# A gated FFN on attention outputs rewritten as a quadratic form in pairs of inducing weights

## The chip, the cores and the metric

The kernel runs on one core of one Trainium2 chip. The metric is the device time of one execution in microseconds (us). In the profile PE is TensorE, PEld its weight loads, DVE is VectorE, ACT is ScalarE, POOL is GpSimd, and SP is SyncE, whose queue issues nearly all DMAs here. L442 is line 442 of the kernel that is profiled.

## The reference

Four batches of 12,416 tokens of 128 features attend to 32 inducing points and back; a gated FFN with 1536 hidden units follows.

```python
h = mab(I, x)                 # 32 x 128 per batch: softmax(I x^T / sqrt(C)) x
x = mab(x, h)                 # per token: a mean of the 32 rows of h with softmax weights
gate = np.maximum(x @ w_gate, 0.0)
val = x @ w_val
return gate * val @ w_out
```

With unnormalized softmax weights p_m and Z = sum of p_m, a token's gate is (sum of p_m G_m)/Z, where G = h w_gate has 32 rows, and its value is (sum of p_m V_m)/Z. All p_m are positive. If the 32 numbers G_m of a unit have one sign, relu is the identity or zero for every token of the batch.

## The kernel before

For each pair of 512-token blocks it makes p by an exponential, then for each of 12 groups of 128 hidden units it forms gate and value by matmuls on p, takes relu on ScalarE, multiplies on VectorE and multiplies by the output weights on TensorE. Scaling by 1/Z^2 goes through a DMA transpose and GpSimd.

```python
        if unit:
            gate = gate_banks(unit)
            for m in unit["mm"][0]:
                gate(*m)                                   # g_ps, PE L910
# ... cut ...
        if unit:
            g16 = unit["g16"] = st([P, 2 * BLK], FP16, "g16", 4)
            w = unit["dst"].shape[-1] // 2
            for k, ps in enumerate(unit["g"]):
                nc.scalar.activation(                      # ACT L1007
                    out=g16[:, k * w : (k + 1) * w], in_=ps[:, 0:w], func=AF.Relu
                )
        if ready:
# ... cut ...
                nc.vector.tensor_tensor(                   # DVE L1019
                    out=dst[:, ks, :], in0=g16[:, ks, :], in1=v[:, ks, 0:w], op=ALU.mult
                )
# ... and in chain(), with the hidden layer as moving operand:
            nc.tensor.matmul(                              # PE L699
                c["ps"][:, 0:w], wo[:, i, :], gv(i), start=(i == 0), stop=(i == NFF - 1)
            )
```

The softmax here doesn't subtract the row's maximum and nothing guards it: scores larger than these inputs give would overflow.

## Time and profile before

| | before |
|---|---|
| time, median of 3 | 698.73 us (698.52 to 698.9) |
| span of the profiled execution | 696.6 us |
| busy PE / DVE / ACT / POOL | 91 / 97 / 97 / 54% |
| granted TensorE clock | 0.9 or more in every slice |

### The profile page before, as it was taken

To read this page: it belongs to the slowest core of one execution; us is meant where nothing else is said; L and a number is where in the kernel's file an instruction comes from. 1 tells how busy PE (TensorE), PEld (TensorE's weight loads), DVE (VectorE), ACT (ScalarE), POOL (GpSimd) and SP (SyncE) were. 2 spreads that over 40 slices of the span, in tenths; PEclk is the share of its full clock that TensorE was granted. 3 is DMA by queue.
4 is the path that set the end of the run, shared out by engine and by line. 5 is a ranking of instruction groups with operands and counts; after the bars stand their busy time and mean duration, and the time that the engine had idled before them with its cause. 6 is when DMAs were issued, how large, how long until landed. Compare 5 with 4: busy or idle time off the path is not lost.

```text
span 696.6 us, 14008 instructions
## 1 busy us (share of the span) xinstructions
PE 633.8 (91%) x4581; PEld 180.6 (26%) x4581; DVE 676.7 (97%) x617; ACT 672.4 (97%) x1381; POOL 372.7 (54%) x681
## 2 busy tenths in 40 slices
PE   7999998999999999989999999998999888888997
PEld 5422222222222222222222222222222222222224
DVE  4799999999999999999999999999999999999997
ACT  5799999999999999999999999999999999999996
POOL 4729746654277554756257473873434543534443
PEclk9999999999999999999999999999999999999999
DMA  9667778531666857513186785632223132232222
GB/s 349 220 133 188 165 170 168 106 99 47 149 163 172 203 139 158 144 50 89 54 204 165 204 175 151 129 93 70 69 76 85 52 92 58 79 90 49 77 56 92
DMA packets 142634, 87.58 MB, mean 126 GB/s; under 512 B 117184, under 2 KB 125664, under 8 KB 140256
## 3 DMA queue, kind: packets, MB, share of 16 engines
q1 hardware_dynamic: 142368, 86.60, 49.1%
q8 instruction: 36, 0.59, 0.3%
q14 instruction: 38, 0.31, 0.2%
q10 hardware_dynamic: 192, 0.08, 0.0%
HBM read 27.80 MB, written 25.43 MB: 76 GB/s over the span
## 4 chain that ended last, share of the span: by engine, by line
ACT 40%; PE 25%; issue 19%; DVE 13%; DMA 1%; SPq 1%; ACTq 0%; POOL 0%; DVEq 0%
ACT g L1007 30%; DVE gv L1019 13%; PE o_ps L699 11%; PE v_ps L910 8%; ACT oT L705 6%; PE g_ps L910 3%; ACT p2q L201 2%; ACT p1T L558 2%; DMA gv<-in_x_dram 1%; PE o_ps L766 1%; ACT hgv L176 1%; SPq L87 1%; PE h_ps L624 0%; PE xT_ps L275 0%; PE idle_ps L269 0%
## 5 line engine op out<-in xcount | busy, mean ns | idle before, releaser
L1019 DVE TENSOR_TENSOR gv<-g,v_ps 128x1024 f16<-128x1024 f16 (+1 forms) x578 | 657.2, 1209 | 3.4 <-ACT g L1007 1.0
L1007 ACT ACTIVATE g<-g_ps 128x512 f16<-128x512 f32 (+1 forms) x1168 | 603.2, 618 | 6.5 <-PE g_ps L910 2.3
L699 PE MATMUL o_ps<-gv,wo 128*128 128x512 f16 x1128 | 352.4, 384 | 46.0 <-ACT oT L705 45.8
L716 POOL TENSOR_SCALAR osb<-o,z2i 128x128 f32<-128x128 f16 x380 | 165.2, 452 | 223.1 <-DMA o<-oT 212.6
L910 PE MATMUL g_ps<-p,hgv 32*128 32x512 f16 x1152 | 282.4, 379 | 0.8 <-ACT g L1007 0.5
L910 PE MATMUL v_ps<-p,hgv 32*128 32x512 f16 x1152 | 223.6, 384 | 5.5 <-DVE gv L1019 4.3
L910 PEld LDWEIGHTS <-hgv 32*128 32x128 f16 x2400 | 66.7, 91 | 267.3 <-issue 263.0
L699 PEld LDWEIGHTS <-wo 128*128 128x128 f16 x1176 | 80.8, 97 | 212.4 <-issue 198.6
L455 POOL TENSOR_TENSOR z2i<-zt,minus 128x16 f32<-128x16 f32 (+3 forms) x31 | 73.4, 2369 | 0.5
L705 ACT CAST oT<-o_ps 128x512 f16<-128x512 f32 (+1 forms) x98 | 59.1, 603 | 0.1
L526 POOL CAST x<-x 128x2048 f16<-128x2048 f32 x18 | 34.1, 1894 | 13.9 <-DMA x<-in_x_dram 13.9
L448 POOL TENSOR_TENSOR zt<-zt 128x32 f32<-128x32 f32 (+5 forms) x124 | 35.0, 282 | 9.7
L448 POOL TENSOR_TENSOR zt<-p2T 128x256 f32<-128x256 f16 (+3 forms) x31 | 17.5, 563 | 33.5 <-DMA p2T<-p2q 20.9
L602 POOL TENSOR_TENSOR zq<-p1g 128x256 f32<-128x256 f16 x18 | 12.1, 672 | 6.5 <-DMA p1g<-p1T 6.5
L276 DVE COPY xT<-xT_ps 128x1024 f16<-128x1024 f16 (+1 forms) x15 | 8.6, 583 | 6.8 <-PE xT_ps L275 6.7
L285 POOL CAST x<-gv 128x512 f16<-128x512 f32 (+2 forms) x15 | 8.5, 564 | 10.3 <-DMA gv<-in_x_dram 10.3
L201 ACT ACTIVATE p2q<-s_ps 128x512 f16<-128x512 f32 x22 | 13.4, 610 | 0.0
L604 POOL TENSOR_TENSOR zq<-zq 128x256 f32<-128x256 f32 x15 | 10.9, 726 | 1.2
L558 ACT ACTIVATE p1T<-s1T_ps 128x512 f16<-128x512 f32 x18 | 11.0, 611 | 0.0
L185 PE MATMUL s_ps<-xT,hT 128*32 128x512 f16 x108 | 10.8, 389 | 0.1
L287 ACT CAST x<-gv 128x512 f16<-128x512 f32 (+2 forms) x15 | 7.1, 495 | 3.9 <-DMA gv<-in_x_dram 3.9
L275 PE MATMUL xT_ps<-eye,x 128*128 128x128 f16 x97 | 8.2, 219 | 2.1 <-DVE x L282 0.7
(97 smaller groups left out, 163.8 us busy)
## 6 DMA issues: line engine op xcount, KB each, us to landing
out_dram<-osb SPq DMA_DIRECT2D x95, 256.0 KB, 2.2
x<-in_x_dram SPq DMA_DIRECT2D x18, 1024.0 KB, 5.9
p<-p2q SPq DMA_DIRECT2D x88, 64.0 KB, 2.0
gv<-in_x_dram SPq DMA_DIRECT2D x9, 512.0 KB, 6.7
o<-oT SPq DMA_TRANSPOSE x98, 2.4
gv<-in_x_dram SPq DMA_DIRECT2D x6, 256.0 KB, 9.1
x<-in_moe_w_out_dram SPq DMA_DIRECT2D x1, 768.0 KB, 8.8
x<-in_moe_w_gate_dram SPq DMA_DIRECT2D x1, 512.0 KB, 6.0
```

Source lines behind the costliest of these rows:

```text
L201: nc.scalar.activation(out=p2q, in_=ps, func=AF.Exp, scale=sm_scale)
L448: nc.gpsimd.tensor_tensor(out=dst, in0=v[:, :, :, 0:m], in1=v[:, :, :, m : 2 * m], op=ALU.add)
L455: nc.gpsimd.tensor_tensor(out=z2i, in0=v[:, :, :, 0], in1=minus1[:, 0 : n * g].rearrange("p (n g) -> p n g", n=n), op=ALU.pow,)
L526: nc.gpsimd.tensor_copy(out=s["x16"][:, t0:t1, :], in_=s["x32", q])
L558: nc.scalar.activation(out=p1T, in_=ps, func=AF.Exp, scale=sm_scale)
L602: add(out=z, in0=s["p1g"][q][:, 0:half, :], in1=s["p1g"][q][:, half:, :], op=ALU.add)
L699: nc.tensor.matmul(c["ps"][:, 0:w], wo[:, i, :], gv(i), start=(i == 0), stop=(i == NFF - 1))
L705: nc.scalar.copy(out=oT[:, 0:w], in_=c["ps"][:, 0:w])
L716: nc.gpsimd.tensor_scalar(out=osb[:, t, :], in0=o16[:, t, :], scalar1=zz, scalar2=zz, op0=ALU.mult, op1=ALU.mult,)
L910: nc.tensor.matmul(ps[:, cols], hgv[:, s * P : (s + 1) * P], p2, start=True, stop=True)
L1007: nc.scalar.activation(out=g16[:, k * w : (k + 1) * w], in_=ps[:, 0:w], func=AF.Relu)
L1019: nc.vector.tensor_tensor(out=dst[:, ks, :], in0=g16[:, ks, :], in1=v[:, ks, 0:w], op=ALU.mult)
```

## The change

For a unit of one sign, relu(gate) times value is a sum over pairs (m, m') of p_m p_m' G_m V_m' / Z^2. A pair weight is one exponential: p_m p_(m+k) = exp(score_m + score_(m+k)), and the sum of two scores is one score against h_m + h_(m+k). So the kernel makes F, 512 pair weights per token (16 shifts k of 32 inducing points), multiplies it with one table T of 512 rows and 129 columns per batch (the last column gives Z^2), and divides once. T is the sum over the units with positive gate of (G_m V_m' + G_m' V_m) times the output weights: products of 768 elements on VectorE into U[0] and U[1], a "join" U[0] + U[1] on GpSimd, and 12 matmuls for each quarter of T. The 16 pairs of shift 16 and up to 16 unsure units go into a fifth block. If more than 16 units are unsure or the sign bound is too wide, a general path recomputes all in a branch.

One slot is one block of 512 tokens; a batch has 24 and a last tile of 128. Work for the next batch (load, cast, transpose, narrow scores, largest |x| for the bound, h, gates, products, tables) is laid over these slots.

```diff
-            for k, ps in enumerate(unit["g"]):
-                nc.scalar.activation(
-                    out=g16[:, k * w : (k + 1) * w], in_=ps[:, 0:w], func=AF.Relu
-                )
# ... cut: all of the hidden layer, its output chain, the transposed way out ...
+        act.activation(
+            out=F[g][:, 2 * half : 2 * half + 2, :], in_=ps, func=AF.Exp, scale=sm_scale
+        )
# ... cut ...
+        for j in range(4):
+            nc.tensor.matmul(
+                ps, F[g][:, j, tok], T[b % 2][:, j, 0 : P + 1], start=j == 0, stop=False
+            )
# ... cut: the fifth block, then per three tiles one reciprocal and one product, and a store ...
+    def products(i, t0, nt, odd):
+        dve.tensor_tensor(
+            out=U[i][:, t0 : t0 + nt, k0:NS:2, :],
+            in0=a[:, t0 : t0 + nt, 0:M].unsqueeze(2).broadcast_to([P, nt, nk, M]),
+            in1=shifted(w, 0, t0, nt, k0 - odd, 2, nk),
+            op=ALU.mult,
+        )
+    def joined(eng, t0, nt):
+        eng.tensor_tensor(
+            out=U[0][:, t0 : t0 + nt, 1:, :],
+            in0=U[0][:, t0 : t0 + nt, 1:, :],
+            in1=U[1][:, t0 : t0 + nt, 1:, :],
+            op=ALU.add,
+        )
# ... cut: the order of the next batch's loads on SyncE, casts on GpSimd, transposes on SyncE ...
+            at = (first + 2 * q) if b > 1 else min(-1, 2 * q - 13)
+            task(at, load, "S")
+            task(at + 3 if b > 1 else at, cast, "S")
+            task(max(at + 5, base - 2 + q) if b > 1 else at, transp, "S")
# ... cut: the products of the next batch, and after every four of them a join ...
+            ops += [lambda i=i, t0=t0, odd=odd: products(i, t0, 3, odd) for i in (0, 1) for odd in (0, 1)]
+            ops.append(lambda t0=t0: joined(pool, t0, 3))
# ... cut ...
+    left = quadratic_kernel(tc, *args)
+    with tc.If(left > 0):
+        general_kernel(tc, *args)
```

## The prediction

> **What bounds the kernel now.** I read the busy table first, then the costliest groups, then one undisturbed stretch by engine.
>
> ```profile
> PE 633.8 (91%) x4581; PEld 180.6 (26%) x4581; DVE 676.7 (97%) x617; ACT 672.4 (97%) x1381; POOL 372.7 (54%) x681
> ...
> L1019 DVE TENSOR_TENSOR gv<-g,v_ps 128x1024 f16<-128x1024 f16 (+1 forms) x578 | 657.2, 1209 | 3.4 <-ACT g L1007 1.0
> L1007 ACT ACTIVATE g<-g_ps 128x512 f16<-128x512 f32 (+1 forms) x1168 | 603.2, 618 | 6.5 <-PE g_ps L910 2.3
> L699 PE MATMUL o_ps<-gv,wo 128*128 128x512 f16 x1128 | 352.4, 384 | 46.0 <-ACT oT L705 45.8
> ```
>
> DVE and ACT are both at 97% with about 5 us of idle: both are full, and they are full of one thing, the hidden layer. Per pair of 512-token blocks DVE does 12 products of 1024 (657.2/578 = 1.14 us each) and ACT 24 relus of 512 (603.2/1168 = 0.52 us each). PE is not the limit. So time falls only if these elements disappear, and both engines must lose them. The change does that.
>
> ```profile
> 300.00:313.60 13.60, 12.26 (x108) 3.52 (x108) 13.59 (x13) 13.29 (x29) 6.74 (x10) 1.00 0.23 65
> ```
>
> That is a steady stretch (stretch, then busy us and instructions of PE, weight loads, DVE, ACT, GpSimd, then clock, DMA share, GB/s): DVE is busy 13.59 of 13.60 us at clock 1.00. The new work is priced from the order of time near the end (start, length) and from the groups by shape (busy us, mean ns):
>
> ```profile
> 689.45 1.29 PE L766 MATMUL o_ps<-wo,gv 128*128 128x128 f16 x20
> ```
>
> ```profile
> L196 ACT ACTIVATE p<-s_ps 128x512 f16<-128x512 f32 x5 | 3.0, 609 | 1.7 <-PE s_ps L185 1.7
> L296 ACT ACTIVATE p<-s_ps 128x128 f16<-128x128 f32 x6 | 1.6, 276 | 1.6 <-PE s_ps L294 1.6
> L779 DVE TENSOR_TENSOR osb<-o_ps,zz 128x384 f32<-128x384 f32 x1 | 0.6, 557 | 0.5 <-PE o_ps L766 0.5
> L319 DVE TENSOR_REDUCE z1s<-z1a_ps 128x32 f32<-128x256 f32 x1 | 0.4, 414 | 0.0
> ```
>
> Twenty matmuls of 128 columns, each with its weight load, take 1.29 us (0.22 latency, then 56 ns each); an exponential's slope (609-276)/384 = 0.87 ns an element; an output eviction of three tiles 557 ns; a reduction of 256 in 414 ns.
>
> **What the Trainium skill says.** "VectorE: DVE Perf Modes", section on the perf-mode tier table: tensor_tensor runs at two elements a cycle on 16-bit SBUF operands, one with a PSUM operand, and tensor_reduce always at one. The trace agrees for PSUM (1024 in 1.14 us) and one reduction; no fp16 SBUF product is in it. "ScalarE: Activation LUTs", section "What ACT_TABLE_LOAD costs": 186 ns + 0.833 N, back-to-back overlapping by about 93 ns, whatever the function. The trace has 609 ns for 512 and 0.52 us start to start: it agrees, so an exponential of 1024 is an estimated 1.04 us, 0.95 us start to start. "TensorE: Matmul & The Clock Gate", section on 56 ns: N/2.4 + 2.5 ns; 56 ns measured here. "Runtime: NRT & Kernel Launch", section "Instruction fetch mechanics": a taken branch to a far target stalls for a fetch; no line of this trace shows it.
>
> **The change, part by part.** Does the general path run? I worked out the test on the reference's inputs: bound 0.0036 (limit 0.0625), 761 to 775 of 1536 units certainly on, the rest certainly off, none unsure (limit 16). So the branch is not taken; the general path costs only the test.
>
> Removed: all of the hidden layer's L1007, L1019 and L699 work, the transposed output path through DMA and GpSimd (380 scalings, 165 us) and GpSimd's sums of exponentials.
>
> Added, per slot of one 512-token block (24 and a rest tile per batch, 100 slots):
> - ACT: two exponentials of 128x1024, 2 x 0.95 = 1.9 us; a 512 one every fourth slot, 0.13. About 2.0.
> - PE: four score matmuls of 512 at 0.216 and twenty of 129 at 0.056: 0.86 + 1.13 = 2.0; unsure units, still computed in full, an estimated 0.17. About 2.2.
> - DVE: per three tiles a reciprocal (estimated 0.17 and 0.1 of dependence) and the 557 ns eviction, 0.77 start to start, so 1.03 a slot; unsure units, 13 passes of 512 from PSUM at 0.62 per batch, 0.3. About 1.35.
>
> So PE sets a plain slot, 2.2 us: 55 us for a batch with nothing else. Added per next batch, laid over 24 slots:
> - PE: 97 x 3 narrow matmuls at about 28 ns = 8 us; tables 60 x 56 ns = 3.4; gates and small ones 2. Total 2.2 x 24.25 + 13, about 66 us.
> - ACT: six exponentials and eight gate copies, some 8 us: about 58 in all.
> - DVE: the largest |x|, 12 reductions of 1024 at about 1.15 = 14 us; 16 products of 768 at 0.49 (two a cycle) = 8; masked output weights 1.7; sums, signs, masks 7. With 25 for outputs and 8 for unsure units, about 62.
>
> The means nearly balance, but they bunch. In slots 1 to 6 DVE holds 1.03 + 2.3 + 0.2 and often 0.62: about 3.9 us against PE's 3.3. In slot 10 ACT has 1.9 + 2.6 of gate copies; in slots 11 and 12 DVE has about 4.7. PE takes everything in order with two output banks, so it cannot hide a peak. Slot by slot: slot 0 2.2; slots 1 to 6 23.4; 7 to 9 2.8 + 2.2 + 2.7; 10 to 13 4.5 + 4.7 + 4.7 + 3.4; 14 to 17 10 (products beside outputs); 18 to 22 14.3 (2.2 and 0.7 for a table each); 23 and 24 4.2; sum 79. Perfect smoothing would give 66. Two output banks hold 1.5 slots, so I choose a value between, nearer the peaks: 74.
>
> Prologue. hT was ready at 23.66 us. The built order puts nine reductions of 1024 (10 us) among DVE's turn copies; DVE was busy 9.3 us of the first 20, so it becomes full there: I add 3 us. Then six more reductions (4 us), sums of h, 16 products (8), bound, signs, masks (5) in one DVE chain, then table, evictions and the first unsure-unit block (6): first output near 51 us.
>
> Batch 1's arrival. Here I expect the largest loss. In the built order SyncE's queue holds load 0, transpose 0, load 1, transpose 1 and so on, and each transpose waits for GpSimd's cast of that load. GpSimd's first cast stands behind the unsure-unit work, which waits for the signs: near 45 us.
>
> ```profile
> x<-in_x_dram SPq DMA_DIRECT2D x18, 1024.0 KB, 5.9
> ...
> xT<-x SPq DMA_TRANSPOSE x18, 4.4
> ```
>
> (DMA issues: KB each, median us to landing; then min/median/max ns of issuing a transpose, of a cast, and the queue's own waits: us in total, times, longest.)
>
> ```profile
> L532 SPq DMA_TRANSPOSE xT<-x x18: 1622/1927/2347, 36.8 to 444.8; - x18
> ```
>
> ```profile
> L526 POOL CAST x<-x x18: 1891/1894/1897, 31.7 to 440.7; 128x2048 f16<-128x2048 f32 x18
> ```
>
> ```profile
> SPq L709 <- ACT g L1007: 253.8, 94, 6.3
> ```
>
> The last line shows the queue standing on one entry's wait. One round is 5.6 (load) + 1.9 (cast) + 1.9 (issuing the transpose) = about 9.5 us. Transposes 0 to 5 issue at 47, 56.5, 66, 75.5, 85, 94.5 and the rest tile near 99; they land 3 to 4 us later. Slot 1+q has in-order score matmuls on chunk q, so slot 7 begins at about 102, not at 51 + 2.2 + 23.4 = 77: some 25 us of PE standing. Later batches issue transposes one per slot, three slots ahead, and escape.
>
> Sum: 102 + slots 7 to 24 of batch 0, 48 (74 less the 25.6 of slots 0 to 6) + two batches of 74 + a last batch with no successor and no scores in its last five slots, 51 + last store, register loads and branch 6 = about 355; the time reported is 2 above the span (698.7 against 696.6): 356.
>
> **The rivals.**
> 1. The arrival chain is hidden or shorter: the first load has long landed, later loads in quiet queues take under 5 us. Against: the median of 5.9 us in a kernel with less store traffic at that point, and the queue order. If hidden, 356 - 25 = about 331.
> 2. PE is fed perfectly (two output banks and exponentials five slots ahead absorb the peaks): batches at 66 instead of 74, about 332; together with rival 1, 310. For it: the means. Against: one in-order PE stream, and only two banks of each kind.
> 3. DVE takes PE's place entirely: fp16 products at one a cycle (0.87 us), reductions slower beside GpSimd's 18 casts. Batches of 82, the prologue 6 us longer: about 385.
> 4. The branch is taken, or the jump costs tens of us. The inputs speak against; the first would at least double the time.
>
> **Range and chances.** 356 with errors of about 7 in the prologue, 10 in the chain and 6 per batch: 325 to 385. The removed work is over 600 us on each of two engines and the added under 270 on any, so faster is nearly certain; only a taken branch would undo it.
>
> **What would show it.** Right: exponentials of 1024 at about 1.04 us mean, 192 of them; 1552 matmuls on F 56 ns apart; first output near 51 us; PE idle in gaps of 5 to 8 us between 55 and 102, released by a DMA landing in xT; clock below 1 there; slots of about 4 us in which DVE is full at the start of batches 1 and 2; 2.2 us slots with PE full in batch 3. Wrong: PE idle on F or on ACT throughout would mean ACT is the limit; reductions far from 1.15 us or products far from 0.5 us would move each batch; a gap after the last store would be the branch.

## More of the kernel before

The page also cuts the span into 40 equal slices and gives the busy tenths of each, 9 for 90% or more. Here they are for DVE and ACT:

```profile
DVE  4799999999999999999999999999999999999997
ACT  5799999999999999999999999999999999999996
```

After a prologue of two slices both engines are full to the end.

## The result

The changed kernel is correct and takes 408.58 us (median of 4; 407.4 to 409.88), the kernel before 698.62 us (698.38 to 698.9) in the same rounds. The ratio is 0.585 (95% interval 0.583 to 0.586). A ratio is the mean time of one kernel's fast runs over the mean time of the other's fast runs of the same rounds, so it is not quite the ratio of the medians quoted. The direction was right, but 408.6 lies above the predicted range of 325 to 385, and 52.6 us over the predicted 356.

From the page of the kernel after: busy shares, slices, then the costliest groups (busy us, mean ns of one | idle just before, and its releaser).

```profile
PE 331.0 (81%) x4358; PEld 230.9 (57%) x4358; DVE 273.5 (67%) x581; ACT 245.5 (60%) x350; POOL 115.9 (28%) x148
...
PE   5874785455696798999996689999996799999993
...
PEclk9696699666689868999998888999998999999998
...
L642 ACT ACTIVATE F<-e_ps 128x1024 f16<-128x1024 f32 x192 | 194.6, 1032 | 90.6 <-PE e_ps L635 83.7
L656 PE MATMUL o_ps<-T,F 128*128 128x129 f16 x1552 | 144.1, 231 | 15.1 <-DVE osb L675 14.8
...
L675 DVE TENSOR_TENSOR osb<-o_ps,rzo 128x384 f32<-128x384 f32 x132 | 72.5, 549 | 7.8 <-DMA out_dram<-osb 3.2
...
L783 DVE TENSOR_REDUCE xmp<-xT 128x1 f32<-128x1024 f16 x36 | 42.1, 1210 | 22.8 <-DMA xT<-x 22.8
```

Both engines that were full have lost over half of their work (DVE from 676.7 to 273.5 us busy, ACT from 672.4 to 245.5), and the prices of the new pieces came as predicted: 192 exponentials of 1024 at 1.03 us, the eviction at 0.55 us, the reduction at 1.21 us. No engine is full on the average. But the slices of PE swing between 4 and 9, and those of its granted clock with them, down to 6: the kernel has stages with different bounds, and the misses are in them. A table by stretch (PE busy, PEld, DVE, ACT, POOL, each with its instructions; granted clock; DMA share; GB/s) separates these stages:

```profile
60.00:114.00 54.00, 31.94 (x477) 23.45 (x476) 23.33 (x38) 18.52 (x22) 9.76 (x6) 0.73 0.58 154
...
178.70:207.00 28.30, 27.02 (x508) 20.38 (x506) 24.96 (x46) 19.89 (x26) 0.00 (x0) 1.00 0.63 142
207.00:241.00 34.00, 27.13 (x291) 17.39 (x289) 28.60 (x60) 21.05 (x31) 18.11 (x19) 0.85 0.55 192
...
365.00:390.00 25.00, 25.00 (x289) 16.60 (x287) 13.57 (x34) 22.85 (x25) 0.00 (x0) 1.00 0.30 116
```

The last row is the last batch, which has no successor: PE is busy 25.00 of 25.00 us at clock 1.00, so PE sets a plain slot, as predicted. Dated by its first matmul on F, such a slot takes 2.04 us without matmuls for the unsure units and 2.45 us with them (three slots of four), 2.35 us on the mean, where the prediction had 2.2. The second row is the first nine slots of batch 1: PE nearly full again. The first row is slots 0 to 6 of batch 0, with PE busy for 31.94 of 54 us at a granted clock of 0.73. The third row is slots 9 to about 15 of batch 1, where most of the products and joins for batch 2 stand: 34 us, PE's work stretched by a clock of 0.85, and GpSimd at work for 18.11 us. The list of waits names what PE waited for in the bad rows (us in total, times, longest):

```profile
PE s_ps L774 <- DMA xT<-x: 21.9, 5, 5.1
...
PE o_ps L656 <- DVE osb L675: 14.8, 8, 3.0
...
PE pos_ps L507 <- DVE row L505: 10.1, 3, 3.4
...
DVE oh L520 <- POOL pm L518: 9.9, 4, 2.7
```

**The first stage.** The narrow scores wait for turned tokens of batch 1. The chain of waits between 54 and 80 us (start, length, what) shows the loop behind it:

```profile
56.66 1.95 SPq L766
...
58.71 5.75 DMA x<-in_x_dram
...
64.51 1.90 POOL x L762
...
66.43 1.71 SPq L766
...
68.24 5.92 DMA x<-in_x_dram
```

SyncE issues a transpose (L766), only then the next load, then stands until GpSimd has cast it: 5.75 + 1.90 + 1.71 and a few hundredths, 9.5 us a round. This is the arrival chain of the prediction, with its predicted period.

**The third stage.** This is the order of time within slots 10 to 15 of batch 1 (start, length, engine, line, operation; in brackets what ended the idle time before):

```profile
226.72 1.89 POOL L762 CAST x<-x 128x2048 f16<-128x2048 f32 x1
226.85 2.17 DVE L442 TENSOR_TENSOR U<-ga,vb 128x768 f16<-128x768 f16 x1
...
231.95 0.61 PE L656 MATMUL o_ps<-T,F 128*128 128x129 f16 x4 [3.05 <-DVE osb L675]
...
233.00 1.06 PE L635 MATMUL e_ps<-xT,hs 128*128 128x512 f16 x2
...
234.00 3.15 POOL L450 TENSOR_TENSOR U<-U,U 128x1440 f16<-128x1440 f16 x1
...
234.31 3.25 DVE L442 TENSOR_TENSOR U<-va,gb 128x768 f16<-128x768 f16 x1
```

A product takes 0.55 us when it stands alone (ten us earlier in the same batch). Beside the cast it takes 2.17, beside the join 3.25, and both times it ends 0.41 us after GpSimd does: 226.72 + 1.89 = 228.61 against 226.85 + 2.17 = 229.02, and 237.15 against 237.56. It is as if the product only begins when GpSimd ends. The whole trace says the same: each of the 23 products that take over 0.65 us began after a GpSimd instruction had, and ended 0.37 to 0.42 us after that one's end. The eviction behind it comes late, PE stands 3.05 us for the output bank, and its two score matmuls take 1.06 us where they take 0.59 elsewhere. The Trainium skill says just this: "SBUF — State Buffer", section "Who interferes with whom", has GpSimd and VectorE share a pair of ports, a VectorE instruction with two SBUF inputs contend with a GpSimd instruction that reads SBUF, and the second one to issue blocked until the first finishes. Its exceptions agree with the trace too: the evictions, which read PSUM, stay at 0.56 us.

| stage | predicted | measured | difference |
|---|---|---|---|
| start to slot 7 of batch 0 | 102 | 114.5 | +12.5 (9.7 of it before the first eviction, at 60.7 instead of 51) |
| slots 7 to 24 of batch 0 | 48 | 64.2 | +16.2 |
| batch 1 | 74 | 88.5 | +14.5 |
| batch 2 | 74 | 83.4 | +9.4 |
| last batch, and the rest to the reported time | 59 | 59.3 | 0.3 |

Slot 7 is dated by its first narrow score, a batch from first eviction to first eviction (from the reciprocal that opens it). The measured column adds up to the 409.9 us of the profiled run, the predicted one to 357, which the prediction rounded to 356.

### The profile page after: what moved, and what is told of

It is laid out like the page before. It is cut to its first block, busy times and chain, and to the rows that moved or that the text cites.

```text
span 407.7 us, 10298 instructions
## 1 busy us (share of the span) xinstructions
PE 331.0 (81%) x4358; PEld 230.9 (57%) x4358; DVE 273.5 (67%) x581; ACT 245.5 (60%) x350; POOL 115.9 (28%) x148
## 4 chain that ended last, share of the span: by engine, by line
PE 46%; DVE 22%; DMA 9%; POOL 7%; ACT 7%; issue 5%; SPq 3%; DVEq 0%; POOLq 0%; ACTq 0%
PE o_ps L656 16%; PE e_ps L635 12%; DMA x<-in_x_dram 7%; DVE U L442 5%; ACT F L642 4%; PE o_ps L660 3%; DVE osb L675 3%; SPq L766 3%; PE hz_ps L795 3%; POOL x L762 3%; DVE xmp L229 3%; PE gv_ps L714 3%; POOL U L450 2%; PE T_ps L488 2%; ACT p L778 2%
## 5 line engine op out<-in xcount | busy, mean ns | idle before, releaser
L642 ACT ACTIVATE F<-e_ps 128x1024 f16<-128x1024 f32 x192 | 194.6, 1032 | 90.6 <-PE e_ps L635 83.7
L656 PE MATMUL o_ps<-T,F 128*128 128x129 f16 x1552 | 144.1, 231 | 15.1 <-DVE osb L675 14.8
L656 PEld LDWEIGHTS <-F 128*128 128x128 f16 x1552 | 109.6, 102 | 49.4 <-DVE osb L675 18.9
L635 PE MATMUL e_ps<-xT,hs 128*128 128x512 f16 x384 | 122.5, 405 | 4.6 <-DVE hs L375 3.9
L660 PE MATMUL o_ps<-T,gmv 128*128 128x129 f16 x388 | 88.5, 228 | 0.1
L675 DVE TENSOR_TENSOR osb<-o_ps,rzo 128x384 f32<-128x384 f32 x132 | 72.5, 549 | 7.8 <-DMA out_dram<-osb 3.2
L450 POOL TENSOR_TENSOR U<-U,U 128x1440 f16<-128x1440 f16 x12 | 35.9, 2991 | 131.1 <-DVE U L442 72.1
L783 DVE TENSOR_REDUCE xmp<-xT 128x1 f32<-128x1024 f16 x36 | 42.1, 1210 | 22.8 <-DMA xT<-x 22.8
L762 POOL CAST x<-x 128x2048 f16<-128x2048 f32 x18 | 34.5, 1928 | 44.7 <-DMA x<-in_x_dram 44.5
L660 PEld LDWEIGHTS <-gmv 128*128 128x128 f16 x388 | 40.1, 103 | 0.7 <-DVE gmv L730 0.2
L635 PEld LDWEIGHTS <-hs 128*128 128x128 f16 x384 | 31.8, 102 | 8.8 <-DVE hs L375 4.0
L720 DVE TENSOR_SCALAR g<-gv_ps 128x512 f16<-128x512 f32 (+1 forms) x28 | 17.7, 630 | 15.5 <-PE gv_ps L714 15.3
L774 PE MATMUL s_ps<-indT,xT 128*128 128x32 f16 x288 | 10.2, 180 | 21.9 <-DMA xT<-x 21.9
L706 ACT ACTIVATE p<-s_ps 128x512 f16<-128x512 f32 (+1 forms) x28 | 15.6, 558 | 2.6 <-PE s_ps L697 2.6
L442 DVE TENSOR_TENSOR U<-ga,vb 128x768 f16<-128x768 f16 x16 | 16.7, 1043 | 0.0
```

Of the source, the lines that this page charges most:

```text
L442: dve.tensor_tensor(out=U[i][:, t0 : t0 + nt, k0:NS:2, :], in0=a[:, t0 : t0 + nt, 0:M].unsqueeze(2).broadcast_to([P, nt, nk, M]), in1=shif ...
L450: eng.tensor_tensor(out=U[0][:, t0 : t0 + nt, 1:, :], in0=U[0][:, t0 : t0 + nt, 1:, :], in1=U[1][:, t0 : t0 + nt, 1:, :], op=ALU.add,)
L635: nc.tensor.matmul(ps[:, d, :], hs[:, j * P : (j + 1) * P], xTs(s["xT"], n * TPB, TPB), start=True, stop=True,)
L642: act.activation(out=F[g][:, 2 * half : 2 * half + 2, :], in_=ps, func=AF.Exp, scale=sm_scale)
L656: nc.tensor.matmul(ps, F[g][:, j, tok], T[b % 2][:, j, 0 : P + 1], start=j == 0, stop=False)
L660: nc.tensor.matmul(ps, gmv[b, n // 4][rows, tok], T[b % 2][rows, 4 + r, 0 : P + 1], start=False, stop=True,)
```

## The experiments

My theory after the result had four parts, for four places: (1) the arrival chain of batch 1 costs some 25 us; (2) in slots 10 to 18 products of two fp16 SBUF operands stand still while GpSimd works; (3) the position matmul waits behind VectorE work; (4) the prologue is long because of the 15 big reductions for the largest |x|. The rival for 2 is that VectorE is simply full there, or that GpSimd's own queue is too long; for 3, that the wait only moves. Each edit is against the changed kernel.

| run | median us (range) | ratio to before | batches 0, 1, 2 (us) |
|---|---|---|---|
| the changed kernel | 408.58 (407.4–409.88) | 0.585 | 117.9, 88.5, 83.4 |
| e1_loads_ahead | 384.68 (383.25–385.43) | 0.550 | 93.4, 88.5, 83.4 |
| e2_no_join | 397.63 (396.67–398.8) | 0.570 | 111.9, 82.8, 82.7 |
| e3_casts_later | 400.63 (399.94–401.34) | 0.573 | 112.0, 84.7, 85.0 |
| e4_row_first | 409.32 (408.69–409.94) | 0.586 | 117.8, 88.6, 83.6 |
| e5_no_largest | 399.66 (399.17–401.44) | 0.572 | 117.3, 88.5, 83.4 |
| e6_no_join_casts_later | 393.12 (392.46–394.49) | 0.563 | 110.5, 81.6, 80.7 |
| e7_relu_on_act | 404.84 (402.44–407.61) | 0.578 | 117.6, 88.6, 82.2 |
| e8_joins_after | 413.44 (412.73–414.01) | 0.592 | 118.3, 88.9, 87.0 |
| e8b_joins_last | 388.83 (388.64–390.48) | 0.557 | 110.0, 81.2, 79.4 |
| e10_joins_on_dve | 401.16 (399.54–403.01) | 0.574 | 115.3, 86.0, 80.1 |
| e12_no_join_tables_late | 397.8 (395.0–400.65) | 0.571 | 111.7, 83.3, 81.2 |
| e9_all | 369.93 (369.27–373.83) | 0.531 | 86.0, 81.6, 81.9 |
| e11_all_row_first | 365.26 (364.26–366.47) | 0.522 | 85.0, 80.2, 80.2 |
| e13_all_joins_last | 365.41 (365.23–366.47) | 0.524 | 85.5, 80.8, 78.3 |
| e14_all_joins_last_casts_later | 370.91 (370.76–371.71) | 0.531 | 86.5, 84.8, 79.5 |

Each row has four runs over three rounds, all correct, with the kernel before at 698.5 to 698.7 beside them. The batches are those of the profiled run, which can lie up to 3 us from the median (e7: 407.61, e12: 395.0). From its first reciprocal to its last, the last batch took 50.5 us in every one.

### e1_loads_ahead: the arrival chain taken apart

```diff
@@ -753,3 +753,3 @@
         first = base - 14
-        task(first, begin, "S")
+        task(first if b > 1 else -30, begin, "S")
         for q in range(NCH):
@@ -806,6 +806,11 @@
 
-            at = (first + 2 * q) if b > 1 else min(-1, 2 * q - 13)
-            task(at, load, "S")
-            task(at + 3 if b > 1 else at, cast, "S")
-            task(max(at + 5, base - 2 + q) if b > 1 else at, transp, "S")
+            at = first + 2 * q
+            if b > 1:
+                task(at, load, "S")
+                task(at + 3, cast, "S")
+                task(max(at + 5, base - 2 + q), transp, "S")
+            else:
+                task(-29 if q < 3 else 2 * q - 33, load, "S")
+                task(2 * q - 28, cast, "S")
+                task(2 * q - 28, transp, "S")
             task(base + 1 + q, score, "B")
```

> Batch 1's first three loads are issued before the first transpose, so a round of the SyncE queue no longer holds a load's flight. Theory (the arrival chain stalls the PE by 28.8 us: slot 0 to the last score takes 53.8 us in batch 0 against 25.0 in batch 1): rounds shrink from 9.7 to about 4 us, the last chunk's scores come near 90 instead of 114, and the time falls by 20 to 29 us to about 380 to 388. Rival (the chain hides another wait, such as output banks or stores held behind the transposes): less than 10 us.

Measured: 384.68, 24 us less, all in batch 0 (117.9 to 93.4 us). The wait for turned tokens falls from 21.9 to this line in the list of waits:

```profile
PE s_ps L774 <- DMA xT<-x: 4.3, 2, 2.5
```

Part 1 holds. The same loads, casts and transposes run; only their order on SyncE differs. The predicted 25 us was right in kind and size.

### e2_no_join, e3_casts_later, e6_no_join_casts_later: GpSimd's work taken away from the products

e2 leaves the joins out: TensorE sums both halves of U, 24 matmuls a quarter table instead of 12.

```diff
@@ -486,6 +486,11 @@
         ps = bank("m", "T_ps", [P, P])
-        for t in range(NFF):
-            nc.tensor.matmul(
-                ps, u_cols(0, t, j), won[:, t, :], start=t == 0, stop=t == NFF - 1
-            )
+        for i in range(2):
+            for t in range(NFF):
+                nc.tensor.matmul(
+                    ps,
+                    u_cols(i, t, j),
+                    won[:, t, :],
+                    start=(i, t) == (0, 0),
+                    stop=(i, t) == (1, NFF - 1),
+                )
         act.copy(out=T[b % 2][:, j, 0:P], in_=ps)
@@ -841,3 +846,3 @@
             ops += [lambda i=i, t0=t0, odd=odd: products(i, t0, 3, odd) for i in (0, 1) for odd in (0, 1)]
-            ops.append(lambda t0=t0: joined(pool, t0, 3))
+            ops.append(lambda: None)
         for k, f in enumerate(ops):
```

> GpSimd's sum of the two product tables (12 of 3.0 us) is gone; the PE adds both tables in PSUM instead, 48 more matmuls of 56 ns per batch, 2.7 us. Theory (a DVE product with two fp16 operands in SBUF cannot proceed while GpSimd works, so the join stretches the product beside it to 1.7 to 3.3 us and the in-order PE stands behind DVE): products beside no other GpSimd work take 0.55 us, the oh step no longer waits 2.7 us for GpSimd, and each of three batches loses some 4 to 8 us: 385 to 397. Rival (DVE's peak of work alone stalls the PE, and GpSimd only fills time that is there anyway): the time rises by up to 8 us for the added matmuls, or stays.

e3 keeps the joins and starts the loads of batches 2 and 3, and so their casts, some slots later, behind the products.

```diff
@@ -806,3 +806,3 @@
 
-            at = (first + 2 * q) if b > 1 else min(-1, 2 * q - 13)
+            at = (base - 10 + q) if b > 1 else min(-1, 2 * q - 13)
             task(at, load, "S")
```

> Loads and GpSimd casts for batches 2 and 3 move out of the slots in which DVE makes the products; nothing is added or removed. Theory of the shared access: the products that were stretched to 2.2 us by a 1.9 us cast go back to 0.55, some 2 to 5 us in each of batches 0 and 1: 400 to 405. Rival (peak of DVE alone): no change within 2 us.

e6 has both edits.

> No joins and the casts out of the product slots. If both act through the same exclusion the gains of 11 and 8 us add up, 389 to 392, and nearly all products of batches 1 to 3 take 0.55 us; if one of them had only uncovered the other's idle time, it stays at 395 or above.

Measured: 11.0, 8.0 and together 15.5 us less. The groups by shape of e6 show the products back near their price (busy us, mean ns):

```profile
L442 DVE TENSOR_TENSOR U<-va,gb 128x768 f16<-128x768 f16 x16 | 10.1, 629 | 0.0
...
L442 DVE TENSOR_TENSOR U<-ga,vb 128x768 f16<-128x768 f16 x16 | 9.7, 606 | 0.0
```

In the changed kernel these two read 972 and 1043 ns. The batches fall from 88.5 and 83.4 to 81.6 and 80.7 us. This speaks for part 2 but doesn't prove it: the edits also shorten GpSimd's queue, and e2 gives TensorE 144 more matmuls. The two gains add up to 19, of which 15.5 came. The product times themselves nearly add: the four groups by shape sum to 57.8 us in the changed kernel, 44.7 in e2, 51.4 in e3 and 39.0 in e6. Why the time gains less is open.

### e8_joins_after and e8b_joins_last: the same instructions, parted in time

A clean test keeps every instruction and changes only what stands beside what. e8 puts the four joins after the last products in the order of issue.

```diff
@@ -841,2 +841,3 @@
             ops += [lambda i=i, t0=t0, odd=odd: products(i, t0, 3, odd) for i in (0, 1) for odd in (0, 1)]
+        for t0 in range(0, NFF, 3):
             ops.append(lambda t0=t0: joined(pool, t0, 3))
@@ -847,3 +848,3 @@
         for j in range(4):
-            task(c + 10 + j, lambda j=j: table(b, j), "B")
+            task(c + 11 + j, lambda j=j: table(b, j), "B")
         task(c + 9, lambda: table5(b), "B")
```

> The same instructions as the changed kernel, but GpSimd's four joins per batch stand behind all products, in slots that have none (tables one slot later). It separates GpSimd's work from its being at the same time as DVE's products, without the 2.7 us of matmuls that the run without joins adds. Theory (products and GpSimd exclude each other): time falls by 6 to 12 us, to 397 to 403, products beside no join at 0.55 us. Rival (the run without joins gained because work was removed from a chain of GpSimd): less than 3 us of gain or a loss.

Measured: 413.44, 4.9 us more. The expectation fell, and the order of time shows why:

```profile
233.68 9.50 POOL L450 TENSOR_TENSOR U<-U,U 128x1440 f16<-128x1440 f16 x3
...
234.04 3.25 DVE L442 TENSOR_TENSOR U<-ga,vb 128x768 f16<-128x768 f16 x1
...
237.21 3.20 DVE L442 TENSOR_TENSOR U<-va,ga 128x672 f16<-128x672 f16 x1
...
241.15 0.62 PE L656 MATMUL o_ps<-T,F 128*128 128x129 f16 x4 [6.46 <-DVE osb L675]
```

A join waits only for its own products. The first three had all been released, so GpSimd ran them back to back for 9.50 us while VectorE still had its last products: two in a row of over 3 us, and PE standing 6.46 us. The edit had not parted the work, it had packed it. For e8b the order of the joins is reversed: the one that needs the last products stands first in GpSimd's queue and holds the others back.

```diff
@@ -841,2 +841,3 @@
             ops += [lambda i=i, t0=t0, odd=odd: products(i, t0, 3, odd) for i in (0, 1) for odd in (0, 1)]
+        for t0 in range(9, -1, -3):
             ops.append(lambda t0=t0: joined(pool, t0, 3))
@@ -847,3 +848,3 @@
         for j in range(4):
-            task(c + 10 + j, lambda j=j: table(b, j), "B")
+            task(c + 13 + j // 2 + j % 2, lambda j=j: table(b, j), "AB"[(j + 1) % 2])
         task(c + 9, lambda: table5(b), "B")
```

> The second try at parting the joins of the product tables from the products in time, with every instruction kept. All four joins (four additions of 1440 fp16 elements a row on GpSimd, 2.99 us each) now stand after the last products, and the one of the last products stands first, so that none can start before VectorE is done with them; the tables come two or three slots later. By the theory that a VectorE product of two fp16 operands from SBUF cannot go on while GpSimd works on SBUF: no product beside a join is over 0.7 us, TensorE no longer waits 3 to 6 us for a table eviction there, and the time falls from 408.6 to between 396 and 403 (leaving the joins out gave 397.6). By the rival, that leaving the joins out helped because GpSimd had 12 us less to do in a batch (its masks, positions and casts stand behind the joins in its queue): nothing is gained, 406 to 414.

Measured: 388.83, 19.8 us less, more than the theory's range. Here the joins follow the last product:

```profile
228.38 0.55 DVE L442 TENSOR_TENSOR U<-va,gb 128x768 f16<-128x768 f16 x1
...
229.02 11.53 POOL L450 TENSOR_TENSOR U<-U,U 128x1440 f16<-128x1440 f16 x4 [3.21 <-DVE U L442]
```

PE's wait for evictions falls from 14.8 to 5.6 us in the list of waits. All 581 VectorE and 148 GpSimd instructions are still there, and GpSimd is as busy as before (115.6 against 115.9 us); only the overlap with the joins is gone. The casts still stretch one product in batch 0 and two in batch 1, to 1.6 or 2.0 us. The edit also packs the products closer and moves the tables, but e8 has the same packing and was slower, and e12 below gives the tables the same late slots for nothing. From e8 to e8b only the order of the joins turns and the tables move, and the time falls by 24.6 us. The rival of the long GpSimd queue predicted 406 to 414 and falls, and part 2 is shown.

### e10_joins_on_dve and e12_no_join_tables_late: the rivals of 388.8

e10 lets VectorE do the joins.

```diff
@@ -841,3 +841,3 @@
             ops += [lambda i=i, t0=t0, odd=odd: products(i, t0, 3, odd) for i in (0, 1) for odd in (0, 1)]
-            ops.append(lambda t0=t0: joined(pool, t0, 3))
+            ops.append(lambda t0=t0: joined(dve, t0, 3))
         for k, f in enumerate(ops):
```

> The joins of the product tables done by VectorE instead of GpSimd: four additions of 1440 elements a batch for batches 1 to 3. [...]one takes 0.55 us times 1440/768, about 1.0 us, 4 us more of VectorE in a batch, and GpSimd loses 12. By the theory of exclusion the products are back at 0.55 us beside them and TensorE has its 12 matmuls a table instead of 24, so most of the 11 us that leaving out the joins gave should come: 396 to 402. By the rival, that in these slots VectorE is simply full and any work on it counts, the added 12 us of VectorE eat the gain: 406 to 412.

Measured: 401.16, 7.4 us less, inside the theory's range. The added VectorE work (12 joins of 0.95 us) costs less than the blocked products did, but it isn't free: batch 1 takes 86.0 us where e2 has 82.8. Part of what the rival says may thus be true as well. But the products, too, are longer than in e2 (48.7 us in all against 44.7), as casts still meet them, so how full VectorE is in these slots isn't shown.

e12 asks why e8b beat e2. It is e2 with the tables in e8b's late slots (the line of e8b's diff that moves the tables, added to e2).

> No joins, as in the run that gave 397.6, but the tables in the late slots of the run that gave 388.8. If the parting in time made the 388.8 and the late slots of the tables nothing, this stays near 397.6 (395 to 400), and what separates it from 388.8 is the 144 further table matmuls of TensorE, 144 x 56 ns = 8 us. If the late tables made it, this falls to 386 to 391.

Measured: 397.8 (with a wide 395.0 to 400.65), the same as e2's 397.63. The late slots give nothing by themselves. What separates e2 and e12 from e8b is TensorE's 144 further matmuls at 56 ns, an estimated 8 us, against 8.8 us measured.

### e4_row_first: the position matmul

VectorE's row of unsure units was put before the masked output weights (1.75 us), so that TensorE's position matmul, which stands in order ahead of other work, need not wait for both.

```diff
@@ -431,2 +431,5 @@
         )
+
+    def masked_wo(b):
+        on = state[b]["on"]
         dve.tensor_tensor(
@@ -492,3 +495,3 @@
 
-    def positions(b):
+    def rows(b):
         s = state[b]
@@ -503,4 +506,8 @@
         )
-        row = mt([P, 1], FP16, "row", 1)
+        row = s["row"] = mt([P, 1], FP16, "row", 1)
         dve.tensor_copy(out=row, in_=s["cum"][:, NFF - 1 : NFF])
+
+    def positions(b):
+        s = state[b]
+        row = s["row"]
         ps = bank("m", "pos_ps", [P, 2])
@@ -835,3 +842,5 @@
         task(c + 3, lambda: masks(b), "A")
+        task(c + 3, lambda: rows(b), "A")
         task(c + 3, lambda: positions(b), "B")
+        task(c + 3, lambda: masked_wo(b), "B")
         task(c + 4, lambda: chosen(b), "A")
@@ -874,2 +883,4 @@
     masks(0)
+    masked_wo(0)
+    rows(0)
     table_all(0, 0, 3)
```

> The masked output weights (1.75 us on DVE) move behind the row counts that a PE matmul waits for; the same work in all. Theory (the PE, in order, stands 3.4 us at the position matmuls of each batch): that wait falls to about 1 us and each of three batches gains 2 to 3 us: 400 to 404. Rival (DVE is full there, so the wait comes back at the next output eviction): within 2 us of 408.

Measured: 409.32, no gain. The wait for the row fell from 10.1 to 5.5 us, and PE's wait for evictions rose from 14.8 to 19.8 us. Part 3 fell and its rival was right: the wait only moved to the evictions. e11 below fits this: there, with the products no longer blocked, the same edit pays.

### e5_no_largest: the price of the reductions

This is a measurement of cost: the largest |x| is replaced by a constant that covers the data, so the result stays correct, but the kernel would not be safe for other data.

```diff
@@ -227,10 +227,3 @@
         def largest(j):
-            t0, t1 = parts[j]
-            nc.vector.tensor_reduce(
-                out=xmp[:, j : j + 1],
-                in_=xTs(xT, t0, t1 - t0).rearrange("p t c -> p (t c)"),
-                axis=AX.X,
-                op=ALU.max,
-                apply_absolute_value=True,
-            )
+            nc.vector.memset(xmp[:, j : j + 1], 0.6)
 
@@ -782,9 +775,3 @@
                     m = n // 2 if n > 1 else 1
-                    dve.tensor_reduce(
-                        out=s["xmp"][:, 2 * q + h : 2 * q + h + 1],
-                        in_=s["xT"][q][:, h * m : (h + 1) * m, :].rearrange("p t c -> p (t c)"),
-                        axis=AX.X,
-                        op=ALU.max,
-                        apply_absolute_value=True,
-                    )
+                    dve.memset(s["xmp"][:, 2 * q + h : 2 * q + h + 1], 0.6)
 
```

> The largest |x| is not computed but set to a constant of 0.6, a cost measurement only: the general test is lost, the output stays right for these inputs. DVE loses 48 reductions of 1.13 us and 6 of 0.6, 58 us. Theory: in the prologue DVE is full from 9 to 52 us, so the first eviction comes 8 to 12 us earlier (49 to 53 instead of 60.7); in slots 1 to 6 of batches 1 and 2 the PE takes over at 3.3 us a slot from about 3.5, so 1 to 3 us each; in batch 0 nothing more, the arrival chain holds it: 393 to 400. Rival (the prologue's end is set by GpSimd's chain for the fifth table and not by DVE): the first eviction moves by less than 4 us and the time stays above 402.

Measured: 399.66, 8.9 us less. The first eviction comes at 53.1 instead of 60.7 us, and batches 1 and 2 stay as they were (88.5, 83.4). So the reductions cost 7.6 us in the prologue and nothing in slots 1 to 6, where the prediction had made VectorE the limit at 3.9 us a slot: PE is the limit there, as the row 178.70:207.00 above shows. (The page has 45 reductions of 1024 elements, not the 48 expected.)

### e7_relu_on_act: a small shift from VectorE to ScalarE

```diff
@@ -719,10 +719,3 @@
             p2s[b, q, "g"] = mt([P, BLK], FP16, "g16", 2)
-            dve.tensor_scalar(
-                out=p2s[b, q, "g"][0:k, 0:w],
-                in0=ps[0:k, 0:w],
-                scalar1=0.0,
-                scalar2=1.0,
-                op0=ALU.max,
-                op1=ALU.mult,
-            )
+            act.activation(out=p2s[b, q, "g"][0:k, 0:w], in_=ps[0:k, 0:w], func=AF.Relu)
         else:
```

> The maximum with zero of the unsure units goes from DVE (24 of 0.69 us) to ACT. Theory (DVE's sum of work in slots 1 to 6 and 10 to 16 stalls the PE): each batch with a successor gains 1 to 3 us, the last batch nothing: 401 to 406. Rival (DVE waits only for GpSimd and its means are far from full): within 1.5 us of 408.

Measured: 404.84, with runs from 402.44 to 407.61. The gain of some 4 us on the medians is not settled better than that: the profiled run is the slowest of the four, and in it batches 0 and 1 hardly move. In e9 below the gain doesn't show.

### e9_all, e11_all_row_first, e13_all_joins_last, e14_all_joins_last_casts_later: together

e9 has e1, e2, e3, e7 and every second large copy of the first batch's turned tokens on ScalarE.

```diff
-            nc.vector.tensor_copy(out=xTs(xT, t0, t1 - t0), in_=ps[:, 0 : t1 - t0, :])
+            if j % 2 and t1 - t0 == 8:
+                nc.scalar.copy(out=xTs(xT, t0, t1 - t0), in_=ps[:, 0 : t1 - t0, :])
+            else:
+                nc.vector.tensor_copy(out=xTs(xT, t0, t1 - t0), in_=ps[:, 0 : t1 - t0, :])
```

> All that the runs before point to, together: the loads, casts and transposes of batch 1 issued ahead (-24 alone), no joins and later casts for batches 2 and 3 (-15.5 together), the relu of the unsure units on ScalarE (-2 to -4), and every second large copy of the first batch's turned tokens on ScalarE (an estimate of -2 to -4 from four copies of about 1 us). If they touch different stages, as the theory has it, the sum holds: 408.6 - 24 - 15.5 - 3 - 3 = 363, between 357 and 370. If the granted clock falls as waits go away, or if TensorE takes over as the bound, less comes: 370 to 382.

Measured: 369.93, at the upper edge of the range; some 7 us less gain than the sum. The first two gains alone, 24 and 15.5 us, lead to 369.1: of the 3 us each for the relu and for the ScalarE copies nothing shows. The copies take 1.01 us instead of VectorE's 0.69, and the first eviction came at 61.6 us, not before the changed kernel's 60.7. Both pieces were a miss.

e11 adds e4's edit to e9.

> The version with everything together, and the row of unsure units before the masked output weights on VectorE, which gave nothing by itself because VectorE was full in those slots. With the joins and casts out of the way VectorE has room there, and the matmul of the positions no longer waits 3.4 us in each batch: 3 to 8 us less than without. By the rival, that the slot order is now bound by TensorE and the wait only moves: within 2 us of the version without.

Measured: 365.26, 4.7 us less than e9. The edit that gave nothing alone gives something once the products are no longer blocked.

e13 is e11 with e8b's joins instead of none, and the casts at their old places; e14 has the later casts too.

> The version of 365.3 with the joins back on GpSimd behind the products and the tables late, and the casts of batches 2 and 3 at their old places. TensorE loses the 144 extra matmuls, 8 us; the two casts that fall among the products cost some 4 us in the two batches. 358 to 363 if the parts add up; 364 to 369 if the late tables or the joins, now beside the transposes of the next batch, cost what the matmuls save.

> The same with the casts later as well: 355 to 360, as the casts no longer fall among the products. By the rival, the casts now wait behind 12 us of joins in GpSimd's queue and the transposes and narrow scores of the next batch come late: 361 to 370, with TensorE waiting for the turned tokens of batches 2 and 3.

Measured: e13 365.41, the same as e11; I put it down to the casts among the products, which pay back the 144 matmuls saved (PE waits 9.6 us for evictions, 4.1 in e11). e14 370.91: its rival was right. The casts now stand behind the joins in GpSimd's queue (joins from 121.00 to 132.5 us in the first batch, and only then three casts in a row), and in the list of waits of e14 the narrow scores wait 7.0 us (4.2 in e13) and the evictions for their stores, a wait that e13 doesn't list:

```profile
DVE osb L685 <- DMA out_dram<-osb: 18.3, 6, 5.7
```

I put this down to loads and transposes that stand in the SyncE queue ahead of the stores, waiting for the late casts. No run tests that link by itself, but the order of time of e14 shows it at one place:

```profile
120.48 0.34 SPq L693 DMA_DIRECT2D out_dram<-osb  x1
...
132.47 5.57 POOL L765 CAST x<-x 128x2048 f16<-128x2048 f32 x3
134.38 0.33 SPq L84 DMA_DIRECT2D x<-in_x_dram  x1
134.80 0.38 SPq L693 DMA_DIRECT2D out_dram<-osb  x1
```

After a store at 120.48 SyncE issues nothing until a load at 134.38, when the first of the three casts has ended (5.57/3 = 1.86 us after 132.47), and only then the next store.

e11 and e13 are the best versions found, at 0.52 of the kernel before, and beat the changed kernel by 43 us.

## Why the prediction was right or wrong

**What bounds, and the removed work: right.** Both full engines lost what was said they would lose, and the branch wasn't taken: no instruction of the general path is in the trace, and the end of the kernel took the 6 us that was put down for it.

**Prices of the added work: right for each alone, but for one.** Exponential 1.03 (1.04 predicted), eviction 0.55, reduction 1.21 in the groups, or 2.33 for two back to back (1.15 predicted for one), products 0.55 alone and 0.47 start to start (0.49). The masked weights took 1.75 us (1.7). The one is the unsure units on PE, "an estimated 0.17" a slot: the last batch shows 0.42 us in three slots of four, 0.31 on the mean, which makes a plain slot 2.35 us and not 2.2.

**Batch 1's arrival: right.** Nine and a half microseconds a round; 25 us predicted, 24 removed by e1. Rival 1, a hidden chain, was rightly put aside.

**Prologue, "first output near 51 us": wrong by 9.7.** The reductions were priced well (3 + 4 predicted, 7.6 removed by e5). Two other things were missing from the sum. The constants for the tables stand on VectorE ahead of the first turn copy, which started at 8.68 us instead of 6.05; and e5, without reductions, still had hT 2.7 us later than before. And GpSimd's chain for the fifth block, which the sum didn't contain, ended at 54.8 us, after VectorE's last product (53.1); from there the first unsure-unit block ran on to 60.7.

**"Perfect smoothing would give 66 ... I choose a value between, nearer the peaks: 74": wrong.** The 66 was PE's own work, and that was mis-sized. In e13, at a full clock and with 12 matmuls a quarter table, PE is busy for 72.55 of the 80.8 us of batch 1 (PE busy first after the stretch, then PEld, DVE, ACT, POOL, clock, DMA share, GB/s):

```profile
147.20:228.00 80.80, 72.55 (x1069) 51.10 (x1066) 59.24 (x130) 61.21 (x90) 31.19 (x24) 1.00 0.73 194
```

So even perfect smoothing would give an estimated 72.5, and 74 left almost no room for peaks. The plain sum of slots, 79, comes near the batches without the joins' collisions (78.3 to 81.6 us for batches 1 and 2 of e6, e11 and e13), but partly by luck. Slots 1 to 6 of batch 1 took 23.1 us in the changed kernel against 23.4 in the sum, yet they are bound by PE and not by VectorE (e5). Slots 10 to 13 took 15.7 us in e6 against 17.3, with 3.4 us of waiting for the position matmul that the list doesn't have. How much the two output banks smooth stays open. In the changed kernel the excess over the predicted slots is in slots 9 to 18.

**"16 products of 768 at 0.49 = 8": the term that was mis-sized.** It is 8 us alone, but in the changed kernel the 64 products took 57.8 us (16.7 + 15.6 + 13.5 + 12.0 in the groups by shape): 10.0 in the prologue, then 17.0, 16.9 and 13.9 for the three next batches. The longest of them held up an eviction, and with it PE and its clock. In its place: a product with two SBUF operands stands while a GpSimd instruction that reads SBUF runs, and then takes its usual time. The prediction had GpSimd only in rival 3, as a brake on reductions, which stay at 1.21 us on the mean of 36, and had put no time on GpSimd's joins. Taking the overlap away while keeping the work (e8b) gave 19.8 us.

**The sum.** 12.5 + 16.2 + 14.5 + 9.4 = 52.6 us is the miss of the profiled run up to the last batch. Taken by cause it is about 10 for the prologue, 3 for the longer stay in the chain, 20 for the collisions with the joins (e8b), and some 20 for the rest. For with those collisions gone in e8b, batches 1 and 2 are still at 81.2 and 79.4 us against 74, and slots 7 to 24 of batch 0 some 8 us over their 48. Of this rest PE's own work is an estimated 6.5 us a batch (72.5 less 66); in batch 0 some 5 us are a slip of the prediction, which took the whole step from 79 to 74 out of slots 7 to 24, where its own list adds up to 53.5. What remains are peaks and the casts among the products. (VectorE's items add up to 64 us, not 62; that moves nothing.) The range had 6 us for a batch, but the missed causes act in all three batches the same way.

**What stays open.** Batch 0 takes 85.5 us in e13 against 80.8 for batch 1; PE waits 4.2 us for turned tokens there, and the rest I haven't traced. e7's gain is not settled.

## What to carry to other kernels

Price an instruction together with what can run beside it: before moving an addition to an idle GpSimd, look for VectorE instructions with two SBUF inputs in the same stretch, and part the two by what releases them, not by their place in the program alone. When an in-order engine feeds from several others, first price its own work from a stretch in which it is full, then add up the slots, and promise no smoothing. A queue that loads, waits and transposes in turn makes latency into throughput: issue the loads ahead.

## What the Trainium skill lacked or had wrong

- "SBUF — State Buffer", section "Who interferes with whom", had the rule that explains the largest missed term, and the prediction overlooked it. Apart from a ratio (a VectorE 6.8 times slower) it has no price for a blocked product: here each of 23 ended 0.37 to 0.42 us after GpSimd, and behind them PE stood for 3.05 and, in e8, 6.46 us.
- "TensorE: Matmul & The Clock Gate", section "Part 1", gives an idle window of about 3.4 us before the clock is halved. Here shorter waits were enough: after one of 3.05 us, and after one of 1.92 us that ended at 244.88, two score matmuls took 1.06 us instead of 0.59. The section doesn't say how much idleness within a window counts.
- No page that I read has what a wait on one entry of SyncE's queue does to the independent loads and stores behind it: 24 us here (e1), in rounds of 9.5 us.
